# One transpose for two heads: keys and queries of a head pair turned together and spread by DMAs inside SBUF, halves of the values' products summed by GpSimd

## The chip, the cores and the metric

The kernel runs on one core of one Trainium2 chip. The metric is the device time of one execution in microseconds (us), lower is better. Inputs and output are fp32 arrays in HBM. A measurement of this kernel can tell about 0.2% (1 us) from no change.

## What is computed

Attention with rotary embedding (2 batches, 8 heads, 576 positions, 64 numbers a head), then two feed-forward layers on its 1152 tokens. The change touches the attention alone.

```python
def rotate(x):
    x1, x2 = (x[..., :half], x[..., half:])
    return np.concatenate([x1 * cos - x2 * sin, x1 * sin + x2 * cos], axis=-1)
q_rot, k_rot = (rotate(q), rotate(k))
scores = scale * np.matmul(q_rot, k_rot.transpose(0, 1, 3, 2))
scores = scores - np.max(scores, axis=-1, keepdims=True)
attn = np.exp(scores)
attn = attn / (np.sum(attn, axis=-1, keepdims=True) + 1e-09)
x = np.matmul(attn, v)
h = ((x @ w_a) * (x @ w_b) @ w_out) @ w_in
# ... SoLU and a layer norm over h, then @ w_out of the second layer
```

## The kernel before, in words

**Units and blocks.** A unit is a pair of heads of one batch: 8 units, numbered u = 0 to 7. The 2 x 576 query rows of a unit are 9 blocks of 128: blocks 0 to 3 are the first 512 rows of head 0, blocks 5 to 8 those of head 1, and block 4 holds the last 64 rows of both.

**Numbers in two parts.** TensorE multiplies in a reduced fp32 format, so each operand is written as a high part (a rounded copy, by ScalarE) and a low part (the rest, by a subtraction on VectorE or GpSimd), and a product is summed over the parts. Keys: high and low part stand above each other, 64 + 64 partitions, in `kS`. Queries: the 64 numbers stand twice above each other, once as high part and once as low part (`qS`, two slots). So one product of a block needs two weights (slots) against the same keys, each in two column halves of 288: four matmuls (L354).

**How a unit's keys and queries are made.** SP (SyncE) issues DMAs that load them (`load`, L186), GpSimd rotates them (`rope`, L224), ScalarE and GpSimd split the keys in parts (`k_hi` L262, `k_lo` L267), a DMA inside SBUF doubles the queries (`q_twice`, L242; unit 1 by GpSimd). TensorE turns them: 18 transposes of 128 x 128 a unit (`kA`, `kB` for the keys of the two heads, `qA`, `qB` for the queries, `R` for the last 64 rows; `k_tp` L284, `q_tp` L290). ScalarE copies them out of PSUM (L326, L329, and L305 with the scale for the queries' high part), VectorE makes the queries' low part (L309).

**The rest of a block.** Row maximum on VectorE (L363), exponential on ScalarE (L371), four transposes of the result (L384), high part by ScalarE (L398) and low part by VectorE (L402) into `pT`; the last 64 columns are turned by `t4A`, `t4R`, `t4B` (L408 to L420). The values' product (`pv_some`, L429) gives 128 rows: 64 from the values' high part and 64 from their low part. ScalarE copies the first 64 to SBUF (`pv_act`, L438), VectorE adds the other 64 (`pv_dve`, L443): four pieces a unit. GpSimd multiplies by the inverse row sums, which go through DRAM and come back spread by DMAs (`rs_copy`, L459), and writes the parts of x (`x_mult` L495, `x_lo` L499).

**What sets the order.** Each step has a position in a table (`PLAN`, with `FIRST`, `SECOND`, `THIRD` for units 0, 1, 2 and on), counted in blocks from the unit's start; the steps of all units are sorted by it and issued in that order. Every engine's queue, SP's DMA queue among them, runs strictly in order. The feed-forward stage after it begins near 168 us.

Of the kernel before, what the change touches and what calls it, by code (L numbers as in the profile page):

```python
# [11 lines left out]
F32 = mybir.dt.float32  # L12
# [22 lines left out]
    "qk": -0.38, "max": 0.22, "exp": 0.97, "tp": 2.23, "hi": 2.82, "lo": 3.13, "load_k": -19.75, "load_q": -16.62,  # L35
    "load_v": -7.16, "rope_k": -12.66, "rope_q": -12.07, "q2": -10.16, "k_hi": -12.41, "k_lo": -10.17, "v_hi": -2.37,
# [26 lines left out]
AB = (71.77, 72.72, 73.77, 75.49, 76.04, 76.81, 81.86, 82.31)
W_POS = (62.96, 63.3, 64.79, 65.28, 66.89, 67.84, 75.0, 76.1, 78.8)
# [45 lines left out]
def attention_gated_ffn_solu_ffn(ctx: ExitStack, tc, q, k, v, wa, wb, wo1, wi2, wo2, gln, rope_cs, out):  # L110
# [69 lines left out]
    qS = [ac.tile([P, 2, 1216], F32R, name=f"qS{i}") for i in range(2)]  # L180
    pT = ac.tile([P, 2, 9, S], F32R, name="pT")
    kS = [ac.tile([P, 2, S], F32R, name=f"kS{i}") for i in range(2)]
    kraw, vraw, kd, qd, V, qt, po = {}, {}, {}, {}, {}, {}, {}
    nm, e, sums, ps, tt, x0, rb, t2s = {}, {}, {}, {}, {}, {}, {}, {}

    def load(u, nm_, parts="ABR", eng=nc.sync):  # L186

        b, h0 = u // NP, 2 * (u % NP)  # L190
# [33 lines left out]
    def rope(eng, u, x, nm_, lo=0, hi=NB, steps=(0, 1, 2)):  # L224
# [17 lines left out]
    def q_twice(u, lo=0, hi=NB):  # L242
        dst, src = (qd[u][:, lo:hi, j, :] for j in range(2))
        if u == 1:
            nc.gpsimd.tensor_copy(dst, src)
        else:
            nc.sync.dma_start(out=dst, in_=src)

    def q_first_twice():
        nc.scalar.copy(qd[0][:, 0:5, 0, :], qd[0][:, 0:5, 1, :])  # L250

    def angles_twice():
        for t in (c_sb, s_sb):
            nc.scalar.copy(t[:, 5:9], t[:, 0:4])
# [7 lines left out]
    def k_hi(u, lo=0, hi=NB):  # L262
        if lo == 0:
            kd[u] = at.tile([P, NB, 2, D], F32R, tag="kd", name=f"kd{u}")
        copy(HI["k"] if u else "act", kd[u][:, lo:hi, 0, :], kraw[u][:, lo:hi])

    def k_lo(u, eng, lo=0, hi=NB):  # L267
        t = kd[u][:, lo:hi]
        eng.tensor_tensor(t[:, :, 1, :], kraw[u][:, lo:hi], _raw(t[:, :, 0, :]), op=ALU.subtract)
# [27 lines left out]
    def q_dst(u, piece, a, cols=slice(0, 512)):  # L297
        t = qS[u % 2]
        if piece == "R":
            return heads(t[:, a, 512:768])[:, :, 0:64]  # L300
        c0 = 0 if piece == "A" else 704
        return t[:, a, c0:c0 + 512][:, cols]

    def q_hi(u, piece, src, *cols):
        nc.scalar.activation(q_dst(u, piece, 0, *cols), src, AF.Copy, scale=1.0 / math.sqrt(D))  # L305

    def q_lo(u, piece, src, *cols):
        hi, lo = (q_dst(u, piece, a, *cols) for a in range(2))
        nc.vector.scalar_tensor_tensor(lo, src, 1.0 / math.sqrt(D), _raw(hi), op0=ALU.mult, op1=ALU.subtract)  # L309
# [625 lines left out]
```

## Time and profile before

| | |
|---|---|
| median of 3 runs | 501.88 us (501.58 to 502.71) |
| the profiled execution | 502.1 us; its span is 500.3 us |
| mean granted TensorE clock | 0.997 |
| DVE, ACT, POOL busy over the span | 75%, 54%, 30% |
| attention (units 0 to 7) | about 0 to 168 us |
| two feed-forward layers | about 168 us to the end |
| DMA | 41.72 MB, mean 83 GB/s |

A time of the trace is counted from the span's start. Busy time of PE is that of pipelined instructions, which overlap; the distance from the start of one to the start of the next is what it costs. The profiled execution is 0.2 us over the median.

### The profile page before, as it was taken

Reading aid. Unit: us, or ns where it says so; the run is one execution under the profiler, and the core shown is the slowest. Engines: PE = TensorE matmul, PEld = TensorE weight load, DVE = VectorE, ACT = ScalarE, POOL = GpSimd, SP = SyncE. Lnnn points to the kernel's source line nnn. Section 1 sums busy time; section 2 is a strip of 40 time slices with the busy share of each in tenths; the row PEclk is TensorE's granted clock in tenths of the full one; section 3 lists DMA queues with packets and bytes.
Section 4 is the critical chain, followed back from the end, with each engine's and each line's share of the span. In section 5 each row is a group of like instructions: output and inputs, shape, how many; then the busy total and the mean of one; then the engine's idle time right before and its main releaser. Section 6 shows DMA issues by size and latency. Waiting matters only on the chain.

```text
span 500.3 us, 7965 instructions
## 1 busy us (share of the span) xinstructions
PE 485.2 (97%) x3008; PEld 458.8 (92%) x3008; DVE 374.3 (75%) x603; ACT 268.7 (54%) x564; POOL 150.8 (30%) x118
## 2 busy tenths in 40 slices
PE   7699999999999999999999999999999999999997
PEld 7589999999988999999999999999999988888886
DVE  5589999999999577666756656689789898755551
ACT  3789999999988344343433433342347434222221
POOL 1997999987305002111111221100000000000000
PEclk9999999999999999999999999999999999999999
DMA  4413423424102243222232121263453100000011
GB/s 113 112 50 98 120 53 99 114 57 135 51 25 85 90 134 114 86 84 85 86 100 97 66 95 64 67 228 128 168 170 126 43 0 22 21 23 21 23 42 42
DMA packets 50804, 41.72 MB, mean 83 GB/s; under 512 B 23695, under 2 KB 46798, under 8 KB 50766
## 3 DMA queue, kind: packets, MB, share of 16 engines
q1 hardware_dynamic: 49882, 40.33, 26.5%
q10 hardware_dynamic: 884, 0.89, 0.5%
q8 instruction: 23, 0.38, 0.3%
q14 instruction: 15, 0.12, 0.1%
HBM read 36.92 MB, written 2.39 MB: 79 GB/s over the span
## 4 chain that ended last, share of the span: by engine, by line
PE 79%; DVE 8%; ACT 5%; POOL 4%; DMA 2%; issue 2%; SPq 0%; ACTq 0%; POOLq 0%; DVEq 0%
PE ab L629 28%; PE x L745 15%; PE out L863 10%; PE h L792 10%; PE pv L433 4%; PE s L354 4%; PE t L384 4%; DVE pT L402 2%; DVE nm L363 2%; PE lt L834 2%; ACT e L371 1%; ACT pT L398 1%; DVE x L447 1%; DMA kraw<-in_k_dram 1%; DMA qd<-in_q_dram 1%
## 5 line engine op out<-in xcount | busy, mean ns | idle before, releaser
L629 PE MATMUL ab<-xT,wab 128*128 128x384 f32 x864 | 151.4, 334 | 0.3 <-DVE a L638 0.3
L629 PEld LDWEIGHTS ab<-xT,wab 128*128 128x128 f32 x864 | 149.5, 188 | 0.6 <-DVE a L638 0.6
L745 PE MATMUL x<-gT,wx 128*128 128x384 f32 x432 | 75.2, 334 | 0.0
L745 PEld LDWEIGHTS x<-gT,wx 128*128 128x128 f32 x432 | 74.9, 188 | 0.1
L354 PE MATMUL s<-kS,qS 128*128 128x288 f32 x320 | 59.3, 311 | 3.6 <-ACT e L371 3.6
L106 POOL TENSOR_TENSOR wab<-f,wab 128x1024 fp32r<-128x1024 f32 x11 | 26.4, 2400 | 120.4 <-ACT wab L103 104.5
L371 ACT ACTIVATE e<-s,nm 128x576 f32<-128x576 f32 x72 | 53.5, 744 | 4.7 <-DVE nm L363 4.6
L402 DVE TENSOR_TENSOR pT<-t,pT 128x512 fp32r<-128x512 f32 x72 | 49.6, 688 | 7.6 <-ACT pT L398 6.2
L363 DVE TENSOR_REDUCE nm<-s 128x1 f32<-128x576 f32 x72 | 53.8, 748 | 1.1 <-PE s L354 1.1
L863 PE MATMUL out<-wout,lnT 128*128 128x512 f32 (+1 forms) x240 | 52.7, 372 | 0.0
L820 POOL TENSOR_TENSOR rs<-mv,mhalf 128x1 f32<-128x1 f32 x9 | 5.3, 586 | 154.8 <-DVE mv L818 154.8
L354 PEld LDWEIGHTS s<-kS,qS 128*128 128x128 f32 x320 | 45.9, 190 | 5.7 <-ACT e L371 5.2
L433 PE MATMUL pv<-pT,V 128*128 128x288 f32 x288 | 50.6, 302 | 0.2 <-DVE pT L420 0.2
L863 PEld LDWEIGHTS out<-wout,lnT 128*128 128x128 f32 x240 | 41.3, 189 | 7.4 <-DVE wout L106 0.2
L384 PE MATMUL t<-ident,e 128*128 128x128 f32 x288 | 44.3, 277 | 0.8
L398 ACT CAST pT<-t 128x512 fp32r<-128x512 f32 x72 | 41.8, 581 | 2.5 <-PE t L384 2.0
L433 PEld LDWEIGHTS pv<-pT,V 128*128 128x128 f32 x288 | 41.4, 188 | 0.7 <-POOL xT L501 0.4
L646 DVE TENSOR_TENSOR gT<-a,gT 128x384 fp32r<-128x384 f32 x36 | 23.5, 651 | 21.9 <-ACT gT L645 21.9
L637 ACT COPY a<-ab 128x384 f32<-128x384 f32 x36 | 17.3, 480 | 41.2 <-PE ab L629 40.6
L645 ACT CAST gT<-a 128x384 fp32r<-128x384 f32 x36 | 18.5, 514 | 37.4 <-DVE a L638 37.4
L384 PEld LDWEIGHTS t<-ident,e 128*128 128x128 f32 x288 | 34.0, 142 | 3.3 <-DVE pT L402 2.2
L805 ACT ACTIVATE et<-h,mx 128x1024 f32<-128x1024 f32 x9 | 10.1, 1118 | 47.8 <-DVE mx L804 47.8
(141 smaller groups left out, 739.1 us busy)
## 6 DMA issues: line engine op xcount, KB each, us to landing
raw<-in_moe_w_a_dram SPq DMA_DIRECT2D x12, 512.0 KB
raw<-in_moe_w_b_dram SPq DMA_DIRECT2D x12, 512.0 KB
raw<-in_moe_w_out_dram SPq DMA_DIRECT2D x8, 768.0 KB
raw<-in_moe_w_in_dram SPq DMA_DIRECT2D x8, 512.0 KB
raw<-in_moe_w_out_dram SPq DMA_DIRECT2D x8, 512.0 KB
kraw<-in_k_dram SPq DMA_DIRECT2D x16, 128.0 KB
qd<-in_q_dram SPq DMA_DIRECT2D x16, 128.0 KB
vraw<-in_v_dram SPq DMA_DIRECT2D x8, 256.0 KB
```

Source lines behind the costliest of these rows:

```text
L106: eng.tensor_tensor(self.w[:, 1], _raw(self.t), _raw(self.w[:, 0]), op=ALU.subtract)
L354: nc.tensor.matmul(s[:, c, :KC], qS[u % 2][:, a, off:off + P], kS[u % 2][:, h, c * KC:(c + 1) * KC], start=(m == 0), stop=(m == last),)
L363: nc.vector.tensor_reduce(t, ps[n][:, :, :KC], axis=AX.XY, op=ALU.max, negate=True)
L371: nc.scalar.activation(t.rearrange("p (c n) -> p c n", c=2), ps.pop(n)[:, :, :KC], AF.Exp, bias=nm.pop(n), accum_out=sums[u][:, i:i + 1],)
L384: nc.tensor.transpose(t[:, j, :], e[n][:, j * P:(j + 1) * P], ident)
L398: nc.scalar.copy(hi, src)
L402: nc.vector.tensor_tensor(lo, src, _raw(hi), op=ALU.subtract)
L433: nc.tensor.matmul(o[:, :KC], w[:, h, 4 if m == 8 else m % 4].rearrange("p a d -> p (a d)"), t[:, m, c * KC:(c + 1) * KC], start=(m == 0), ...
L629: nc.tensor.matmul(pab[f, t][:, m, :CW], wf[:, a, m, kk, :], xT[kk][:, xa, t * CW:(t + 1) * CW], start=(kk == a == xa == 0), stop=(kk == 3 ...
L745: nc.tensor.matmul(o[:, :CW], wx[:, a], gT[f // 3, t][:, f % 3, ga], start=(f == 0 and a == ga), stop=(f == NF - 1 and a == 1),)
L792: nc.tensor.matmul(s[:, c], x2T[kk][:, xa, c0:c0 + P], wt["h", kk][:, a, c * 512:(c + 1) * 512], start=(idx == 0), stop=(idx == 11),)
L863: nc.tensor.matmul(o[:, cols], t[:, la, kk, :], w[:, a, cols], start=(kk == la == a == 0), stop=(kk == NK2 - 1 and la == 1),)
```

## The change

For units 1 to 7 the keys and queries of both heads stand side by side (64 + 64 numbers in a row), so that one transpose turns a block of both heads: 4 for the keys (`kt`), 4 for the queries (`qt`), 3 for the last rows (`rt`), 11 in place of 18. The parts are then made from PSUM for both heads at once: high by ScalarE, low by VectorE, for the keys into `kB[0]`, `kB[1]`, for the queries into `qS[u % 2][1]`. The layout that the products need is made by 7 DMAs inside SBUF (`k_move`, 2 for each head; `q_move`, 2 and 1), all issued by SP. Block 4 uses `kB` and `qR` directly: 6 matmuls in place of 8. Two small DMAs (`shift`) bring the last rows of head 1 to the lower partitions. The values' products are copied whole (128 partitions) into `xs`, three DMAs (`x_move`) bring the halves that belong together onto the same partitions, and GpSimd adds them ahead of its multiplication. GpSimd's `k_lo`, ScalarE's `k_hi` and the DMA of `q_twice` are gone for units 1 to 7. Unit 0 keeps its way, with tables and keys in another column order; the last unit keeps VectorE's addition. All positions are new.

```diff
-    "v_lo": 5.8, "kA": (-7.65, -7.05), "qA": (-6.45, -5.8, -4.87), "R": (-1.59, -1.1, -0.66), "kB": (-3.16, -2.58),
-    "qB": (0.13, 0.57, 0.89), ...
+    "load_v": -9.48, "rope_k": -16.68, "rope_q": -10.25, "shift": (-11.47, -9.83), "v_hi": -1.05, "v_lo": 3.4,
+    "kt": (-10.76, -10.2, -8.88), "qt": (-7.29, -6.88, -5.82), "rt": (-5.65, -5.35, -4.19), "k_move": (-3.88, -1.79),
+    "q_move": (-3.26, -0.88), ...
+    "sa": 9.13, "x_move": (11.98, 15.68),
...
+    def shift(u, nm_):
+        t, last = (kraw[u % 2], 9) if nm_ == "k" else (qraw[u % 2], 10)
+        nc.sync.dma_start(out=t[0:64, last], in_=t[64:128, 8])
...
+    def kt_pe(u):
+        o = qt[u, "k"] = bank(f"kt{u}")
+        for n in range(4):
+            nc.tensor.transpose(o[:, n * P:(n + 1) * P], pair(kraw[u % 2], 2 * n), ident)
...
+    def kt_act(u):
+        nc.scalar.copy(kB[0][:, u % 2, 0:REM], qt[u, "k"])
+
+    def kt_dve(u):
+        nc.vector.tensor_tensor(
+            kB[1][:, u % 2, 0:REM], qt[u, "k"], _raw(kB[0][:, u % 2, 0:REM]), op=ALU.subtract
+        )
...
+    def k_move(u, h):
+        own, other = (LOW, HIGH)[h], (HIGH, LOW)[h]
+        t = kS[u % 2][:, h]
+        move(t[own], kB[0][own, u % 2])
+        move(t[other], kB[1][own, u % 2])
+
+    def q_move(u, h):
+        q0_, q1_ = qS[u % 2]
+        if h == 0:
+            move(q0_[LOW], q1_[LOW])
+            move(q0_[HIGH], q1_[LOW])
+        else:
+            move(q1_[LOW], q1_[HIGH])
...
+        else:
+            prods = [(qR[u % 2][:, a], kB[b][:, u % 2]) for a, b in ((0, 0), (0, 1), (1, 0))]
...
+        nc.scalar.copy(xs[u, h][:, c * KC:(c + 1) * KC], po[u, key][:, :KC])
...
+    def x_move(u, h):
+        if h == 0:
+            xs[u, 2] = at.tile([P, S], F32, tag="xs2", name=f"xs2_{u}", bufs=1)
+            nc.sync.dma_start(out=xs[u, 2][LOW], in_=xs[u, 0][HIGH])
+        else:
+            nc.sync.dma_start(out=xs[u, 0][HIGH], in_=xs[u, 1][HIGH])
+            nc.sync.dma_start(out=xs[u, 2][HIGH], in_=xs[u, 1][LOW])
...
     def x_mult(u):
+        x0[u] = xs[u, 0]
+        nc.gpsimd.tensor_tensor(x0[u], x0[u], xs[u, 2], op=ALU.add)
         nc.gpsimd.tensor_tensor(x0[u], x0[u], rb.pop(u), op=ALU.mult)
```

How the order changes, at three places. First SP's queue in the middle of the attention, before: one unit's round from the queries of unit 5 on (`rd`, `rb` are the row sums on their way through DRAM).

```order
L203 DMA qd5_1116<-in_q_dram 128x4x64 x2
L207 DMA qd5_1116<-in_q_dram 128x1x64
L466 DMA rd2_1132<-rr2_1130 9x128
L473 DMA rb2_1134<-rd2_1132 64x576
L474 DMA rb2_1134<-rd2_1132 64x512
L475 DMA rb2_1134<-rd2_1132 64x64
L212 DMA vraw4_1139<-in_v_dram 128x2x256
L217 DMA vraw4_1139<-in_v_dram 64x2x64 x2
L203 DMA kraw6_1304<-in_k_dram 128x256 x2
L207 DMA kraw6_1304<-in_k_dram 128x1x64
L247 DMA qd5_1116<-qd5_1116 128x9x64
```

The same queue with the change: the first 12 rows of a round (unit 3's keys and queries are laid out).

```order
L386 DMA kS1_99<-kB0_100 64x576
L386 DMA kS1_99<-kB1_101 64x576
L386 DMA qS1_0_104<-qS1_1_105 64x1024 x2
L255 DMA kraw0_108<-kraw0_108 64x64
L524 DMA xs0_1_790<-xs1_1_882 64x576
L525 DMA xs2_1_880<-xs1_1_882 64x576
L197 DMA kraw1_109<-in_k_dram 128x4x64 x2
L200 DMA kraw1_109<-in_k_dram 128x1x64
L386 DMA kS1_99<-kB0_100 64x576
L386 DMA kS1_99<-kB1_101 64x576
L197 DMA qraw1_111<-in_q_dram 128x4x64 x2
L200 DMA qraw1_111<-in_q_dram 128x1x64
```

A round before has 14 DMAs. With the change these 12 rows are 15, and ten more follow: L386, L255, L215, L220 x2, L542, L549, L550, L551, L522.

Second TensorE's queue in unit 3, before: `qtkB4`, `qtR4` are transposes for unit 4, `s` the products of queries and keys, `t` the transposes of the exponentials.

```order
L354 MATMUL s31_1184<-kS1_101,qS1_98 128x288 x8
L433 MATMUL pv102_1166<-pT_99,V2_702 128x288 x4
L384 MATMUL t29_1206<-ident_65,e29_1173 128x128 x4
L433 MATMUL pv112_1211<-pT_99,V2_702 128x288 x5
L354 MATMUL s32_1217<-kS1_101,qS1_98 128x288 x4
L433 MATMUL pv112_1211<-pT_99,V2_702 128x288 x4
L384 MATMUL t30_1233<-ident_65,e30_1198 128x128 x4
L354 MATMUL s33_1246<-kS1_101,qS1_98 128x288 x4
L408 MATMUL t4R3_1251<-ident_65,e31_1224 64x128
L286 MATMUL qtkB4_1255<-ident_r_102,kd4_948 128x128 x4
```

With the change, the same unit from its block 2 on.

```order
L416 MATMUL s29_1117<-kS1_99,qS1_0_104 128x288 x4
L354 MATMUL qt4_1122<-ident_65,qraw0_110 128x128 x4
L444 MATMUL t27_1127<-ident_65,e27_1091 128x128 x4
L493 MATMUL pv102_1135<-pT_97,V2_751 128x288 x9
L416 MATMUL s30_1151<-kS1_99,qS1_0_104 128x288 x4
L444 MATMUL t28_1156<-ident_65,e28_1133 128x128 x4
L359 MATMUL rt4_1171<-ident_65,kraw0_108 128x128
L359 MATMUL rt4_1171<-ident_65,qraw0_110 128x128 x2
L416 MATMUL s31_1177<-kB0_100,qRR1_107 128x288 x2
L416 MATMUL s31_1177<-kB1_101,qRR1_107 128x288 x2
L416 MATMUL s31_1177<-kB0_100,qRR1_107 128x288 x2
```

Block 4 (`s31`) goes from 8 matmuls to 6, and the last rows of unit 4 are turned in the middle of unit 3, by three transposes.

Third the start of TensorE's queue, with the change: all of unit 0's transposes (`qtkA0` to `qtqB0`) stand ahead of the first product `s0`, and unit 1's `kt1`, `qt1`, `rt1` stand among unit 0's blocks.

```order
L285 MATMUL qtkA0_204<-ident_r_114,kd0_112 128x128 x4
L291 MATMUL qtqA0_211<-ident_65,qd0_113 128x128 x4
L285 MATMUL qtR0_226<-ident_r_114,kd0_112 128x128
L291 MATMUL qtR0_226<-ident_65,qd0_113 128x128
L285 MATMUL qtkB0_240<-ident_r_114,kd0_112 128x128 x4
L291 MATMUL qtqB0_248<-ident_65,qd0_113 128x128 x4
L416 MATMUL s0_260<-kS0_98,qS0_0_102 128x288 x4
L416 MATMUL s1_268<-kS0_98,qS0_0_102 128x288 x4
L349 MATMUL kt1_275<-ident_65,kraw1_109 128x128 x4
```

Before, `qtkB0` and `qtqB0` stood behind the third product.

## Rows read from the trace of the kernel before

**Rows 1.** Stretches of one unit's length: time, each engine's busy time, clock, DMA share, GB/s
```profile
77.60:95.20 17.60, 17.50 (x142) 16.82 (x141) 16.91 (x30) 17.14 (x44) 16.61 (x14) 1.00 0.35 89
95.20:112.80 17.60, 17.50 (x142) 16.82 (x141) 16.90 (x30) 17.13 (x44) 15.75 (x13) 1.00 0.35 88
```
**Rows 2.** Timeline of PE, first products of units 1 and 7: start, length, engine, line
```profile
31.25 0.69 PE L354 MATMUL s<-kS,qS 128*128 128x288 f32 x4
...
138.60 0.69 PE L354 MATMUL s<-kS,qS 128*128 128x288 f32 x4
```
**Rows 3.** Timeline of PE inside unit 3: transposes and products
```profile
73.14 0.60 PE L292 MATMUL qtqA<-ident,qd 128*128 128x128 f32 x4
73.50 0.77 PE L354 MATMUL s<-kS,qS 128*128 128x288 f32 x4
...
74.77 0.60 PE L384 MATMUL t<-ident,e 128*128 128x128 f32 x4
75.12 1.31 PE L354 MATMUL s<-kS,qS 128*128 128x288 f32 x8
76.28 0.69 PE L433 MATMUL pv<-pT,V 128*128 128x288 f32 x4
```
**Rows 4.** Groups by shape up to 200 us: count, then total busy us and mean ns
```profile
L309 DVE SCALAR_TENSOR_TENSOR qS<-qtqB,qS 128x512 fp32r<-128x512 f32 x8 | 5.5, 692 | 0.8 <-ACT qS L305 0.5
L309 DVE SCALAR_TENSOR_TENSOR qS<-qtR,qS 128x128 fp32r<-128x128 f32 x8 | 2.3, 283 | 0.0
L447 DVE TENSOR_TENSOR x<-pv,tmp3pv 64x288 f32<-64x288 f32 x4 | 1.8, 460 | 0.1
L258 ACT CAST kd<-kraw 128x576 fp32r<-128x576 f32 x7 | 4.7, 669 | 1.5 <-POOL kraw L240 1.5
L269 POOL TENSOR_TENSOR kd<-kraw,kd 128x576 fp32r<-128x576 f32 x7 | 10.0, 1422 | 0.0
L496 POOL TENSOR_TENSOR x<-x,rb 128x576 f32<-128x576 f32 x7 | 10.0, 1424 | 0.5 <-DVE x L447 0.5
```
**Rows 5.** Timeline of POOL: one round of a unit, and a wait for a load
```profile
65.94 1.44 POOL L496 TENSOR_TENSOR x<-x,rb 128x576 f32<-128x576 f32 x1
...
81.86 1.42 POOL L496 TENSOR_TENSOR x<-x,rb 128x576 f32<-128x576 f32 x1
...
109.29 1.43 POOL L233 TENSOR_TENSOR t2q<-qd,s_sb 128x576 f32<-128x576 f32 x1 [1.42 <-DMA qd<-in_q_dram]
```
**Rows 6.** Timeline of SP's queue, one unit's round of issues
```profile
87.39 1.24 SPq L203 DMA_DIRECT2D qd<-in_q_dram  x2
...
89.34 0.41 SPq L466 DMA_DIRECT2D rd<-rr  x1
91.90 0.51 SPq L473 DMA_DIRECT2D rb<-rd  x1
92.47 0.59 SPq L474 DMA_DIRECT2D rb<-rd  x1
...
96.06 1.01 SPq L203 DMA_DIRECT2D kraw<-in_k_dram  x2
97.11 0.55 SPq L207 DMA_DIRECT2D kraw<-in_k_dram  x1
97.77 0.65 SPq L247 DMA_DIRECT2D qd<-qd  x1
```
**Rows 7.** Chain that ended last, 40 to 58 us: a load from issue to landing
```profile
41.49 3.37 DMA qd<-in_q_dram
```
**Rows 8.** Timeline of POOL at the start: unit 1's queries, then unit 0's values
```profile
12.40 1.40 POOL L233 TENSOR_TENSOR t2q<-qd,s_sb 128x576 f32<-128x576 f32 x1
...
21.08 0.72 POOL L260 CAST V<-vraw 128x640 fp32r<-128x640 f32 x1
```
**Rows 9.** Stretches of 2 us in unit 0, columns as in Rows 1
```profile
20.00:22.00 2.00, 0.28 (x2) 0.05 (x1) 0.36 (x1) 0.83 (x2) 2.00 (x3) 1.00 0.42 94
...
24.00:26.00 2.00, 1.53 (x9) 1.05 (x9) 1.97 (x4) 1.20 (x4) 2.00 (x2) 0.50 0.03 8
```

More of the change, by code (lines that the diff above doesn't have):

```diff
@@ L184, in attention_gated_ffn_solu_ffn, with load @@
+    kraw = [ac.tile([P, 10, D], F32, name=f"kraw{i}") for i in range(2)]
+    qraw = [ac.tile([P, 11, D], F32, name=f"qraw{i}") for i in range(2)]
+    kd0 = w0.tile([P, NB * P + 384], F32R, tag="w", name="kd0")
+    qR0 = kd0[:, NB * P:].rearrange("p (a n) -> p a n", a=2)
+    kd0 = kd0[:, :NB * P].rearrange("p (b a d) -> p b a d", a=2, d=D)
+    qd0 = w0.tile([P, NB, 2, D], F32, tag="w", name="qd0")
+    vraw, V, qt, po, xs = {}, {}, {}, {}, {}
     nm, e, sums, ps, tt, x0, rb, t2s = {}, {}, {}, {}, {}, {}, {}, {}
-    def load(u, nm_, parts="ABR", eng=nc.sync):
+    def load(u, nm_):
@@ L206, in load, with load_first @@
-        if "R" in parts:
-            eng.dma_start(out=t[:, 4, :], in_=src[b, h0:h0 + 2, REM:S, :])
+        src, t = (k, kraw[u % 2]) if nm_ == "k" else (q, qraw[u % 2])
+        for j in range(2):
+            nc.sync.dma_start(
+                out=t[:, j:8:2], in_=src[b, h0 + j, 0:REM, :].rearrange("(p c) d -> p c d", c=4)
+            )
+        nc.sync.dma_start(out=t[:, 8], in_=src[b, h0:h0 + 2, REM:S, :])
+    def load_first(nm_, part, eng=nc.sync):
+        src, t = (k, k0) if nm_ == "k" else (q, q0)
+        if part == "R":
+            eng.dma_start(out=t[:, 4], in_=src[0, 0:2, REM:S, :])
+        else:
+            j = "AB".index(part)
+            eng.dma_start(
+                out=t[:, 5 * j:5 * j + 4], in_=src[0, j, 0:REM, :].rearrange("(p c) d -> p c d", c=4)
+            )
@@ L260, in copy, with k_hi, k_lo @@
             {"dve": nc.vector, "pool": nc.gpsimd}[eng].tensor_copy(dst, src)
[L262 to L269, printed above, removed]
+    def k_hi(lo, hi):
+        nc.scalar.copy(kd0[:, lo:hi, 0, :], k0[:, lo:hi])
+    def k_lo(eng, lo, hi):
+        t = kd0[:, lo:hi]
+        eng.tensor_tensor(t[:, :, 1, :], k0[:, lo:hi], _raw(t[:, :, 0, :]), op=ALU.subtract)
     def v_hi(u):
@@ L294, in heads, with q_dst @@
     def heads(ap):
         return ap.rearrange("p (h n) -> p h n", h=2)
-    def q_dst(u, piece, a, cols=slice(0, 512)):
-        t = qS[u % 2]
+    def q_dst(piece, a, cols=slice(0, 512)):
         if piece == "R":
[L300 to L309, printed above, removed]
@@ L315, in qt_pe, with q_lo, q_part, first_pe @@
+    def q_lo(piece, src, *cols):
+        hi, lo = (q_dst(piece, a, *cols) for a in range(2))
+        lo_q(lo, src, hi)
+    def q_part(fn, lo, hi):
+        fn("A", qt[0, "qA"][:, lo:hi], slice(lo, hi))
+    def first_pe(u, key):
         o = bank(f"qt{key}{u}")
         if key == "R":
-            k_tp(o, u, "R")
-            q_tp(o[:, P:2 * P], u, "R")
+            k_tp(o, "R")
+            q_tp(o[:, P:2 * P], "R")
         else:
-            (k_tp if key[0] == "k" else q_tp)(o, u, key[1])
+            (k_tp if key[0] == "k" else q_tp)(o, key[1])
@@ new lines, in move @@
+    def move(dst, src):
+        nc.sync.dma_start(out=_raw(dst), in_=_raw(src))
+    LOW, HIGH = slice(0, 64), slice(64, 128)
+    def k_move(u, h):
[10 more added lines that the diff above has]
+            move(q1_[LOW], q1_[HIGH])
@@ L596, in attention_gated_ffn_solu_ffn @@
             add(plan["load_v"][0], load_v, u)
-            add(plan["rope_k"][0], lambda u: rope(nc.gpsimd, u, kraw[u], "k"), u)
-            add(plan["rope_q"][0], lambda u: rope(nc.gpsimd, u, qd[u][:, :, 1, :], "q"), u)
-            add(plan["q2"][0], q_twice, u)
-            add(plan["k_hi"][0], k_hi, u)
-            add(plan["k_lo"][0], k_lo, u, nc.gpsimd)
+            add(plan["rope_k"][0], lambda u: rope(nc.gpsimd, u, kraw[u % 2], "k"), u)
+            add(plan["rope_q"][0], lambda u: rope(nc.gpsimd, u, qraw[u % 2], "q"), u)
+            add(plan["shift"][0], shift, u, "k")
+            add(plan["shift"][1], shift, u, "q")
+            for h in range(2):
+                add(plan["k_move"][h], k_move, u, h)
+                add(plan["q_move"][h], q_move, u, h)
+            for key, fns in (("kt", (kt_pe, kt_act, kt_dve)), ("qt", (qt_pe, qt_act, qt_dve)), ("rt", (rt_pe, rt_act, rt_dve))):
+                for pos, fn in zip(plan[key], fns):
+                    add(pos, fn, u)
         for key, fn in (("v_hi", v_hi), ("v_lo", v_lo), ("sa", sums_add)):
@@ L604, in attention_gated_ffn_solu_ffn @@
         if u < NU - 1:
+            for h in range(2):
+                add(plan["x_move"][h], x_move, u, h)
             for key, fn in (("x_mult", x_mult), ("x_lo", x_lo)):
@@ L616, in attention_gated_ffn_solu_ffn @@
             for key in keys:
-                for pos, fn in zip(plan[key], (qt_pe,) if u == 0 and key == "qA" else fns):
+                for pos, fn in zip(plan[key], (first_pe,) if u == 0 and key == "qA" else fns):
                     add(pos, fn, u, key)
```

200 lines of the change are left out of this document (109 added, 91 removed), and 19 rows, old and new, of tables (FIRST, PLAN).

## Prediction, made before the changed kernel ran

> **What bounds the kernel now.** I first read the busy time in stretches of one unit's length [rows 1]. In the middle of the attention a unit takes 17.6 us, and PE (17.50), ACT (17.1) and DVE (16.9) are all busy nearly throughout; POOL has 15.75 to 16.6. No single engine is in the way: a unit gets shorter only if all three get less work and nothing else is fuller than the rest. Then I read PE's timeline for two marks [rows 2]: unit 1's first product starts at 31.25 us, unit 7's at 138.60. Six units lie between, 107.35 us or 17.9 each. What comes after 138.60 (the last unit, then the feed-forward layers, PE busy throughout) keeps its work, so I count it unchanged. Third, SP's queue [rows 6], since the change puts much there. The sum is made against the profiled execution, 502.1 us (span 500.3), which is 0.2 over the median of 501.88.
>
> **The change part by part, for one of units 1 to 7.**
>
> *PE.* 18 transposes become 11 and block 4 has 6 products in place of 8. Four transposes take 0.35 to 0.36 us from their start to the next group's (73.14 to 73.50, 74.77 to 75.12), eight products 1.16 (75.12 to 76.28) [rows 3]: 0.09 and 0.145 each. Removed: 7 x 0.09 + 2 x 0.145 = 0.92 us. PE goes from 17.5 to 16.6.
>
> *DVE.* Out go four additions of the halves at 0.46 and the three low parts of the queries, 0.69 + 0.69 + 0.28 [rows 4]: 3.50 us. In come two low parts of 512 columns, one of 128 and one of 64; the last has no row, between nothing and the 0.28 of 128 columns, I take 0.2. That is 1.86. DVE goes from 16.9 to 15.3.
>
> *ACT.* The keys' high part (0.67 [rows 4]) goes, and four copies of 512 columns become two. The four copies of the values' products now read 128 partitions in place of 64 over the same columns; nothing here says that partitions cost time. ACT ends well below PE.
>
> *POOL.* `k_lo` (1.42) goes and the addition of the halves comes, the same form and size as the multiplication beside it (1.42 [rows 4]). A round stays at 15.9 us (65.94 to 81.86 [rows 5]): hidden as long as the unit takes more.
>
> So the engines allow 16.6 us, set by PE; its lower end is POOL's 15.9, if part of PE's 17.5 is waiting that the busy time hides. Six units at 16.6 are 99.6, **7.75 us less** than 107.35.
>
> *SP's queue.* One round of a unit goes from 87.39 to 97.77, 10.38 us, for 13 DMAs, without the doubling of the queries that is dropped. It includes 2.15 in which SP stands still (89.34 + 0.41 to 91.90), because the row sums must land in DRAM before they are read back [rows 6]. The key loads come now in the pieces of the query loads: two take 1.24 in place of 1.01, so 10.6. Then come 12 more: 4 moves of keys, 3 of queries, 3 of x, 2 shifts. None is in the trace. The shortest neighbour is the 0.41 of the row sums plus a gap of 0.05: 0.46. A load with whole rows on both sides takes 0.525 with its gap (96.06 to 97.11 for two), a spread of 64 x 576 takes 0.57 (91.90 to 92.47), others 0.64, and the one DMA inside SBUF 0.65 + 0.05 = 0.70. I take 0.55, between the two rows whose shapes are nearest (whole rows; 64 x 576). A round is then 10.6 + 12 x 0.55 = 17.2 us, 0.6 more than PE's 16.6. This holds for the five units 1 to 5, where all 25 DMAs are issued; from unit 6 on the loads of keys and queries are over. 5 x 0.6 = 3.0 us of lag.
>
> Part of it is absorbed. The first moves of a unit stand 3.47 blocks ahead of its first product (positions -3.88 and -0.41), 6.4 us at 16.6 a unit; four issues (2.2) and a landing like that of the row sums (2.15) leave 2.0 us that SP may be late. So **1.0 us comes back**. The Trainium skill ("DMA: Bandwidth & Descriptors", section "Issuing engines are not separate DMA queues") says that a sequencer's time to start a DMA is usually small against the DMA itself; by that the term would be nothing. The rows speak against it: an issue is 0.4 to 0.65 us.
>
> *Behind the waiting DMAs.* `k_move` waits for ScalarE's and VectorE's parts, `shift` for GpSimd's rotation, `x_move` for the copies of the last values' products. Behind them in the same queue stand the loads of the unit after next, which have a unit of time, and the row sums, for which only POOL waits. I cost these waits at nothing as long as POOL keeps its round.
>
> *The transfers.* The moves carry 64 partitions each. The Trainium skill ("SBUF — State Buffer", section "Door 1: The DMA port swizzle") speaks against such a layout: 64 neighbouring partitions reach half of the ports, 196 GB/s against 328 at 1 MiB. By that, as an estimate, the 262 KB of a query move take 1.3 us in place of 0.8, the 2.0 us of lag allowed become 1.5, and the sum would be 0.5 us worse. No row here shows a transfer by halves of the partitions alone.
>
> *The start.* Unit 1's keys and queries are now turned inside unit 0: block 5 stands behind `rt1`, which waits for the rotation of unit 1 on POOL and for `shift`. POOL's six rotations take 8.7 us (12.40 to 21.08 [rows 8]); with an issue, a landing of 2.15 and three transposes block 5 starts near 24.1. Four blocks at 16.6 / 9 = 1.84 later unit 1 begins, at 31.5, against 31.25 now. I count no difference. At the low end it is a microsecond earlier; at the high end see the rivals.
>
> **Sum:** -7.75 + 1.0 = -6.75 us, 502.1 - 6.75 = **495.3 us**, or 495.1 from the median.
>
> **The rivals.**
> - *SP's queue has room:* at 0.46 an issue the round is 16.1, below PE, and nothing comes back: 494.4 us. For it: several issues of rows 6 are near 0.4 to 0.5. This is also what the skill's rule on issues would give.
> - *The moves land late:* a load took 3.37 us from issue to landing where other transfers stood ahead of it [rows 7]. With that in place of 2.15 the lag allowed is 0.8 and 2.2 come back: 496.5. The skill's halved ports would push the same way. Against: the DMA engines are busy only 0.35 of the time now [rows 1].
> - *POOL waits for the halves:* its addition stands ahead of the next rotations and needs the last `x_move`. If it idles 1.42 us a round, as it does once for a load [rows 5], a unit takes 17.34, and 4.4 us come back: 498.8.
> - *The start loses the clock:* PE stood idle at 20 to 22 us, and the granted clock went to 0.50 by 24 to 26, the 1.2 GHz level, after that idling [rows 9]. The new order has more waiting there (all of unit 0's transposes ahead of its first product, then the wait for `shift`). Three microseconds more are 498.3.
> - *SP's queue is the bound, and the kernel is slower:* if a DMA inside SBUF costs what the only such row does, 0.70 [rows 6], the round is 10.6 + 8.4 = 19.0. 2.4 x 5 - 2.0 = 10.0 come back: 504.4. It decides from the point where the gain is used up, (7.75 + 2.0) / 5 = 1.95 over 16.6, which is 0.66 an issue. For it: 0.64 is the most frequent step in rows 6. Against: those are spreads from DRAM and loads in pieces; the moves are whole rows on both sides, and the doubling of the queries was in 256-byte pieces.
>
> **How the numbers follow.** Forecast 0.34, SP has room 0.18, moves land late 0.10, POOL waits 0.12, start 0.08, SP is the bound 0.18. The predicted time is the forecast's, 495.3. The range takes in the lower engine bound (16.6 to 15.9 in six units, 4.2 us below 494.4, near 490) only in part and most of the last rival: 491 to 502.5, with about 0.07 below and 0.11 above. Within 0.2%, about what can be told from no change (500.9 to 502.9): 0.04 of the last rival, 0.03 of POOL's, 0.02 of the start's, together 0.09. Slower: 0.14, all from the last rival. Faster: 0.77.
>
> **What would show it right or wrong.** Right: unit 1's first product near 31 us, unit 7's near 132, units of 16.6 to 17; DVE clearly less busy than PE in a unit's stretch; SP issuing almost without a break, each new DMA about 0.5 us; the feed-forward part as long as before. Wrong: new issues of 0.65 or more and PE waiting for `kS` or `qS` at a unit's first block (SP is the bound); POOL idle ahead of its addition with a DMA as releaser (POOL); a low granted clock between 10 and 30 us and unit 1 starting after 33 (the start); or a longer time after unit 7's start, which I count as unchanged.

## The result, and the profile after

The changed kernel takes **506.66 us** (median of 4 runs, 505.27 to 507.01) against 501.73 for the kernel before in the same measurements: ratio 1.009, interval 1.0066 to 1.0113. It is slower, where 495.3 was forecast, and outside the range. The profiled execution is one of 507.01 us with a span of 505.2, so the span grew by 4.9 us.

PE's timeline gives the two marks of [rows 2], now:

```profile
33.79 0.43 PE L416 MATMUL s<-kS,qS 128*128 128x288 f32 x2
...
144.96 0.58 PE L416 MATMUL s<-kS,qS 128*128 128x288 f32 x1 [2.95 <-DMA qS<-qS]
```

Unit 1 starts 2.5 us later (33.79 against 31.25), the six units take 111.17 in place of 107.35, and what follows takes 505.2 - 144.96 = 360.2 in place of 361.7. So +2.5 + 3.8 - 1.5 = +4.8, up to rounding the whole difference. The six units take 16.56, 20.35, 18.40, 18.42, 18.42 and 19.02 us.

The stretches of a unit's length, to be read against [rows 1] (columns as there):

```profile
82.40:100.90 18.50, 16.13 (x130) 15.55 (x129) 15.04 (x27) 15.31 (x40) 15.03 (x13) 1.00 0.71 167
100.90:119.00 18.10, 16.35 (x132) 15.78 (x131) 15.26 (x27) 15.57 (x40) 15.69 (x13) 1.00 0.73 171
```

Every engine got the smaller amount of work that was forecast: PE 16.1 to 16.4 (16.6 forecast), DVE 15.0 to 15.3 (15.3), POOL 15.0 to 15.7 (15.9). Yet a unit takes 18.4 us, and the clock is full. So none of the engines is the bound. The DMA share has gone from 0.35 to above 0.7. SP's queue, one round of a unit, tells where the time goes (against [rows 6]):

```profile
82.41 0.59 SPq L522 DMA_DIRECT2D xs<-xs  x1
83.10 1.19 SPq L386 DMA_DIRECT2D kS<-kB  x2
84.34 1.23 SPq L386 DMA_DIRECT2D qS<-qS  x2
85.67 0.73 SPq L255 DMA_DIRECT2D kraw<-kraw  x1
86.51 1.24 SPq L524 DMA_DIRECT2D xs<-xs  x1
87.80 0.59 SPq L525 DMA_DIRECT2D xs<-xs  x1
88.44 1.29 SPq L197 DMA_DIRECT2D kraw<-in_k_dram  x2
...
94.58 0.54 SPq L255 DMA_DIRECT2D qraw<-qraw  x1
...
97.33 0.46 SPq L542 DMA_DIRECT2D rd<-rr  x1
99.16 0.47 SPq L549 DMA_DIRECT2D rb<-rd  x1
...
100.95 0.59 SPq L522 DMA_DIRECT2D xs<-xs  x1
```

From 82.41 to 100.95 are 18.54 us for 25 DMAs, each issued right behind the one ahead. The only pause is 1.37 us (97.79 to 99.16) for the row sums on their way through DRAM. The 12 new DMAs take 8.75 us of it with their gaps, 0.73 each; the 13 old ones 9.79 with the pause. Where nothing lengthens it, the issue of a DMA of 16 KB (L255) takes 0.54, one of 144 KB 0.59, one of 256 KB (`qS`) 0.62 with its gap: its own size hardly matters. Some issues are longer, the first `kraw` (0.73) and the `xs` behind it (1.24); the experiments come back to them. The list of SP's waits, 50 to 125 us, says the same from the other side. The kernel before had this row at the top, loads that wait for a buffer to come free (us in total, times, longest):

```profile
SPq L203 <- PE t L384: 22.8, 4, 7.0
```

That was SP's room, over 5 us a unit; the changed kernel has no such row. What PE waits for in the same stretch:

```profile
PE rt L359 <- DMA qraw<-qraw: 7.3, 4, 3.0
PE s L416 <- DMA qS<-qS: 1.0, 2, 0.7
PE s L416 <- ACT e L431: 1.0, 1, 1.0
```

`rt` are the three transposes of the last rows in the middle of a unit; they wait for `shift`, the 16 KB DMA that stands near the end of SP's round.

### The profile page after: what moved, and what is told of

Read it like the earlier page. It is cut to its first block, busy times and chain, and to the rows that moved or that the text cites. A ratio compares the mean times of both kernels' runs of the same rounds, so it can differ in the third digit from the quotient of the medians.

```text
span 505.2 us, 7965 instructions
## 1 busy us (share of the span) xinstructions
PE 478.7 (95%) x2945; PEld 455.2 (90%) x2945; DVE 364.0 (72%) x582; ACT 257.4 (51%) x542; POOL 150.9 (30%) x121
## 4 chain that ended last, share of the span: by engine, by line
PE 83%; DMA 8%; POOL 4%; ACT 2%; SPq 2%; issue 1%; DVE 0%; POOLq 0%; ACTq 0%; DVEq 0%
PE ab L720 30%; PE x L836 15%; PE out L954 10%; PE h L883 10%; PE s L416 5%; PE pv L493 5%; PE t L444 4%; DMA qraw<-qraw 3%; DMA kraw<-in_k_dram 2%; DMA qS<-qS 2%; PE lt L925 2%; DMA xs<-xs 1%; POOL xs L573 1%; POOL xs L574 1%; ACT e L431 1%
## 5 line engine op out<-in xcount | busy, mean ns | idle before, releaser
L416 PE MATMUL s<-kS,qS 128*128 128x288 f32 x256 | 49.0, 316 | 6.3 <-DMA qS<-qS 4.4
L416 PEld LDWEIGHTS s<-kS,qS 128*128 128x128 f32 x256 | 38.6, 199 | 8.4 <-issue 3.1
L728 ACT COPY a<-ab 128x384 f32<-128x384 f32 x36 | 17.2, 479 | 43.2 <-PE ab L720 42.4
L444 PEld LDWEIGHTS t<-ident,e 128*128 128x128 f32 x288 | 35.2, 143 | 0.9
```

Source lines behind the costliest of these rows:

```text
L416: nc.tensor.matmul(s[:, c, :KC], wq, mk[:, c * KC:(c + 1) * KC], start=(m == 0), stop=(m == len(prods) - 1),)
L444: nc.tensor.transpose(t[:, j, :], e[n][:, j * P:(j + 1) * P], ident)
```

## The experiments

Theory A: SP's time bounds units 1 to 5, so many issues at some 0.6 to 0.7 us whatever they carry, plus what SP stands still. Theory B: the transfers bound, bytes and pieces in flight that land late. Besides, the order on SP's queue could be at fault. All kernels are the changed one with one edit; later ones combine edits. "Six units" is the distance between the two marks in the profiled execution, "on SP" the DMAs of a round.

| run | on SP | median us | ratio to the kernel before | unit 1 | six units |
|---|---|---|---|---|---|
| before | 13 | 501.7 | | 31.25 | 107.35 |
| the change | 25 | 506.66 | 1.009 (1.0066 to 1.0113) | 33.79 | 111.17 |
| e1_x_act | 22 | 507.43 | 1.0104 (1.0082 to 1.0127) | 34.30 | 111.47 |
| e2_three_more | 28 | 517.29 | 1.0305 (1.029 to 1.032) | 34.52 | 120.63 |
| e3_half_bytes | 25 | 499.04 | 0.9946 (0.9929 to 0.9964) | 33.48 | 103.49 |
| e4_merged | 23 | 503.26 | 1.0026 (1.0007 to 1.0045) | 33.54 | 108.86 |
| e5_no_x | 22 | 501.40 | 0.9983 (0.9974 to 0.9993) | 34.32 | 104.19 |
| e6_rd_apart | 25 | 500.39 | 0.9979 (0.9955 to 1.0003) | 34.25 | 103.56 |
| e7_order | 25 | 511.77 | 1.0187 (1.0161 to 1.0214) | 33.16 | 114.49 |
| e8_all | 23 | 499.88 | 0.9953 (0.9928 to 0.9977) | 32.62 | 104.79 |
| e9_whole_rows | 25 | 504.39 | 1.0062 (1.0045 to 1.0079) | 33.11 | 107.83 |
| e10_best | 23 | 500.04 | 0.9967 (0.9947 to 0.9987) | 32.95 | 103.93 |
| e11_x_pool | 22 | 503.86 | 1.0055 (1.0021 to 1.0089) | 33.72 | 112.32 |
| e12_three_act | 25 | 510.07 | 1.0164 (1.0144 to 1.0184) | 34.22 | 114.37 |
| e13_shift | 23 | **495.21** | **0.9878 (0.9857 to 0.9898)** | 32.42 | 100.16 |
| e14_x_act_rd | 22 | 501.30 | 0.9993 (0.9971 to 1.0015) | 33.52 | 101.77 |
| e15_shift_alone | 25 | 509.13 | 1.0148 (1.0133 to 1.0163) | 33.56 | 114.38 |

The profiled execution is one run of several and can lie off the median: 4.7 us above it in e11, about 2 us below it in e9 and e14, within 1.4 us elsewhere. "Issue time" below is the sum of the lengths of a round's issues in the trace, without gaps and pauses, for three rounds in the middle of the attention; in the changed kernel it is 15.3 to 15.9 us.

**Three small DMAs more.**

```diff
+        for i in range(h, 2 * h + 1):
+            nc.sync.dma_start(out=spare[i % 2], in_=ident[0:64, 0:64])
```

> Three DMAs a unit more on SP's queue, each of 16 KB from the identity into a spare tile that nobody reads, beside the moves of the values' halves. Theory A: three issues of about 0.55 us (what the last rows' shift of the same 16 KB takes) lengthen SP's round from 18.5 to about 20.2 us; in the five or six rounds 8 to 10 us more: 514 to 517 us. Theory B: 48 KB beside 3 MB in a unit are nothing: 506 to 508 us.

517.29, 10.6 us more than the change, for 48 KB a unit. SP's rounds (from one `rd` to the next) go, in the middle of the attention, from 18.2 to between 20.1 and 20.5. Theory A is right on the count: 0.6 to 0.8 us an issue with its gap, passed on to the unit in full.

**Half the bytes.**

```diff
-        move(t[own], kB[0][own, u % 2])
+        n = S if u == 1 else KC
+        move(t[own, 0:n], kB[0][own, u % 2, 0:n])
```

(the same for the other three kinds of move)

> From unit 2 on the seven moves of keys and queries carry half their bytes (half the columns of the keys, one of the two slots of the queries; the other half of the tiles keeps an older unit's numbers); as many DMAs at the same places. 0.66 MB less a unit. Theory A: the round stays at 18.4 to 18.5 us and the time at 505 to 508 us. Theory B: landings of 3 to 4 us get shorter by up to a half, units shrink to 17 to 17.5 us: 499 to 502 us.

499.04: here Theory B's number came. Theory A's claim that bytes don't matter falls. SP's queue shows through what they act:

```profile
99.73 0.55 SPq L255 DMA_DIRECT2D kraw<-kraw  x1
100.38 0.54 SPq L526 DMA_DIRECT2D xs<-xs  x1
100.97 0.59 SPq L527 DMA_DIRECT2D xs<-xs  x1
```

The first DMA of `xs` behind the two moves of queries took 1.24 us in the changed kernel (86.51); with half the bytes it takes 0.54, and the shift ahead of it 0.55 in place of 0.73. The issue time of a round falls to 14.3 to 15.1 us, and PE's wait for the shift from 7.3 to 4.7. The pause for the row sums hardly changes (1.1 to 1.3 us, before 1.1 to 1.5). So the two theories are not rivals: what is in flight lengthens SP's round and the landings behind it.

**Fewer issues by merged loads.**

```diff
-        for j in range(2):
-            nc.sync.dma_start(out=t[:, j:8:2], in_=src[b, h0 + j, 0:REM, :]...)
+        nc.sync.dma_start(out=t[:, 0:8].rearrange("p (c j) d -> p c j d", j=2),
+                          in_=src[b, h0:h0 + 2, 0:REM, :]...)
```

> The two loads of 512 rows each (head 0 and head 1) of a unit's keys become one DMA, and so those of its queries: two issues less in a round, the same bytes in the same pieces. Theory A: if an issue costs the same however much it carries, the round falls by 2 x 0.62 = 1.2 us to 17.3: five rounds give 6 us back, 500 to 502 us. If an issue's cost grows with its pieces: unchanged, 506. Theory B: the bytes and pieces are the same, 505 to 507 us.

503.26, 3.4 us less, between the two theories. The issue of a merged load takes 0.66 us where nothing lengthens it, hardly more than one of the two before (0.60 to 0.65), but half of Theory A's gain is missing: the issue time of the 23 is 15.1 to 16.1 us, as long as that of the 25, because issues that are left got longer (two of the merged query loads take 1.40 and 2.03). So SP's round is not a count times a fixed price.

**Larger pieces in the loads.**

```diff
-                out=t[:, j:8:2], in_=...
+                out=t[:, 4 * j:4 * j + 4], in_=...
```

> The loads of a unit's 512 rows of keys and queries write head 0's and head 1's four blocks one after the other in place of alternately, so that a piece is 1 KB in place of 256 bytes; as many DMAs, as many bytes, same places and waits. The blocks that are paired in a transpose are then other rows than the reference pairs. Theory A (SP's issues): nothing changes, 505 to 508 us. Theory B (what is in flight holds up SP and the landings): the small pieces of the loads are what the moves queue behind; landings get shorter, units fall from 18.4 to 17.6 or less as when the moves carried half: 499 to 502 us.

504.39, between the two: the 256-byte pieces cost some 2 us (506.66 - 504.39), not the main part.

**The values' part undone.** `pv_act`, `pv_dve` and `x_mult` as in the kernel before, no `x_move`.

> The values' part of the change is undone (copies of 64 partitions by ScalarE, additions by VectorE, no DMA for the halves, no addition by GpSimd); the keys' and queries' part stays. Three DMAs and 0.43 MB a unit fewer, VectorE 1.8 us a unit more. Theory A (the count of DMAs on SP sets the round): the round falls from 18.4 by 2.0 to 16.4, then VectorE at about 17 us bounds: 499 to 502 us. Theory B (bytes in flight hold up SP and the landings): the 0.43 MB fewer are two thirds of what the halving took off (0.66 MB, 7.6 us less), about 5 us less: 501 to 503 us, with units of 17.7. The values' part as the cause of the loss would show as a time at or below the kernel before.

501.40, in both theories' range, so it does not tell them apart. But VectorE is all but full then, as forecast:

```profile
90.00:110.00 20.00, 19.71 (x154) 18.45 (x152) 19.58 (x35) 18.29 (x48) 16.59 (x14) 1.00 0.66 157
```

DVE is busy for 19.58 of 20 us, and PE for 19.71; a unit takes 17.4 us on average (104.19 / 6). So the room that SP gets back cannot be used much further without the values' part, and on a full SP that part costs more than it brings (506.66 against 501.40).

**The pause taken out.**

```diff
         nc.sync.dma_start(out=d, in_=rr)
+    def rs_back(u):
+        d = rd.pop(u)
...
+            add(9 * u + 14.8, rs_back, u)
```

> Nothing but an order on SP's queue: the three DMAs that spread the row sums stand 4.5 blocks behind the one that writes them to DRAM (behind one move of the values' halves, two of keys, two of queries) in place of right behind it. Theory A (SP's time): SP no longer stands still for 1.4 us in each round; units 1 to 5 go from 18.4 to 17.0, five rounds give 7 back: 499 to 501 us. Theory B (landings): the transfers are the same, 505 to 507 us. If part of the still-stand returns as issues that wait for room: 502 to 504 us.

500.39: 6.3 us less by an order alone, with the same DMAs and bytes. This is Theory A's number, but not quite by its sum. In the profiled execution units 1 to 5 give back 4.4 us (87.75 against 92.15), not 7: in most rounds SP now stands still for 0.8 to 0.9 us ahead of the key moves, and unit 3 takes 19.85 us, with a wait of PE for the shift (2.00) and half the clock behind it. Unit 6 gives another 3.2 (15.81 against 19.02), because there the pause had been 3.9 us, behind 1 MB of feed-forward weights.

**The same three DMAs on other queues.** For ScalarE `nc.scalar` in place of `nc.sync` in `x_move`, for GpSimd `nc.gpsimd`.

> The three DMAs of the values' halves of a unit are issued by ScalarE's queue in place of SP's; bytes, places and waits stay. Theory A (SP's issues are the bound: 25 in a round of 18.5 us, each about 0.6 to 0.7 us whatever its size): SP's round loses the 2.4 us that these three took and falls to about 16.1, PE's work of 16.3 to 16.6 a unit becomes the bound, about 2 us come back in each of units 1 to 5: 496 to 499 us. Theory B (the moves land late because of their bytes and their 64 partitions): the transfers are the same, 505 to 507 us. Rival to both: ScalarE pays 0.5 us an issue in its own queue and holds up the exponentials, above 507.

> The three DMAs of the values' halves are issued by GpSimd's queue in place of SP's, nothing else. They gave nothing when ScalarE's queue issued them. If ScalarE's queue was the reason (each issue held up exponentials behind it): GpSimd has 2 to 3 us a unit to spare, units fall towards 17, 498 to 502 us. If taking issues off SP does not help because the transfers are the limit: 505 to 508 us. If an issue costs GpSimd over 1 us: its 15.5 us of work become over 18.5 and the time 507 us or more.

507.43 and 503.86: nothing, and 2.8 us. In the run with ScalarE SP's round hardly got shorter: the 22 issues left take 14.3 to 15.5 us, against 15.3 to 15.9 for 25, and the pause grew in two of three rounds, here from 1.37 to 2.32 us:

```profile
96.49 0.72 SPq L542 DMA_DIRECT2D rd<-rr  x1
99.53 0.47 SPq L549 DMA_DIRECT2D rb<-rd  x1
```

The small write now stands in flight right behind the same loads. On GpSimd's queue an issue takes 0.53 us, but it waits in order for ScalarE's copies, with the next rotations behind it (this trace is of an execution of 508.61 us, so it shows the loss larger than the median has it):

```profile
85.83 0.53 POOL L524 DMA_DIRECT2D xs<-xs  x1 [3.97 <-ACT pT L476]
86.36 0.52 POOL L525 DMA_DIRECT2D xs<-xs  x1
86.89 1.45 POOL L235 TENSOR_TENSOR t2q<-qraw,s_sb 128x576 f32<-128x576 f32 x1
```

Two more runs were to tell ScalarE's own cost from the pause.

> The three spare 16 KB DMAs a unit of the earlier run, issued by ScalarE's queue in place of SP's. On SP they cost 10.6 us. If only SP's own time counts: 506 to 509 us. If ScalarE pays for an issue: 3 x 0.55 us on its 15.3 us a unit still fits into 18.4, but in the places where TensorE waits for it up to 1 us a unit comes on top, 508 to 512 us. If all queues issue through one place: as on SP, 514 to 517 us.

> Both the values' halves issued by ScalarE's queue (which gave nothing alone) and the row sums' read apart from their write (which gave 6.3 us alone). If SP's round is its issues plus its standing still, and the three issues taken away only made it stand longer for the row sums (2.4 to 3.0 us in place of 1.4): now nothing is left to stand for and units fall to 16.6 to 17, 496 to 499 us. If ScalarE's own cost of an issue was the reason: 500 to 504 us, no better than the row sums apart alone. If the transfers are the limit: 505 us or more.

510.07: an issue is not free on ScalarE's queue, but three cost 3.4 us in place of 10.6. 501.30: with the pause gone, ScalarE's issues add nothing to the row sums apart (500.39). Both fall where ScalarE's own cost was expected. In the profiled executions the last one's six units are 1.8 us shorter than with the row sums apart alone (101.77 against 103.56), but what follows unit 7's start is 1.8 us longer (362.1 against 360.3), so how the two causes share is not settled.

**Two places on SP's queue.**

```diff
-        load(1, "q")
         load(1, "k")
+        load(1, "q")
...
-    for f, loaded, steps in ((0, 54.0, W_POS[:6]), ...
+    for f, loaded, steps in ((0, 48.0, W_POS[:6]), ...
```

> Two places on SP's queue, nothing else: unit 1's keys are loaded ahead of its queries at the start, and the first feed-forward weights (1 MB) are loaded 6 blocks earlier, behind the row sums of unit 4 in place of ahead of those of unit 5. If the start and unit 6 lose what the trace shows (1.0 to 1.5 us by GpSimd's wait for unit 1's keys; 2.4 us by row sums that wait behind the weights): 502 to 504 us. If SP's count alone is behind it: 506 to 507 us.

511.77, 5.1 us worse. The start gained 0.6 (33.16). The weights, 6 blocks earlier, stand in front of unit 6's moves: unit 5 takes 22.8 us, 4.9 of them PE's wait for unit 6's queries. A place on a full queue that looks free is not.

**All of these together**, then with the weights at the start.

> Merged loads, the row sums apart and the two changed places together. Theory A: SP's round is 18.4 - 1.2 - 1.4 = 15.8 us, below TensorE's 16.6; units of 16.6 to 17.0 and the start and unit 6 without their losses: 491 to 495 us, faster than the kernel before. Theory B: transfers stay, units of 17.5 to 18: 498 to 502 us.

> As the kernel with merged loads, row sums apart and unit 1's keys first, but the first feed-forward weights (1 MB) are loaded during the start, ahead of unit 0's values, where the chip moves little, and not in unit 5. If the 20.3 us of unit 5 there came from the weights (the other units take 17.6): 2.5 to 3 us less, 496 to 498 us. If the transfers of the start are held up by them: unit 1 starts later by up to 2 us and the gain is used up, 498 to 500 us.

499.88 and 500.04: both beat the kernel before, but less than Theory A forecast (499.88 lies in Theory B's range), and moving the weights gave nothing. The cause that I had named for the first one's unit 5 (20.3 us) was wrong; PE's timeline shows another, and behind it a stretch of two us:

```profile
110.70 0.33 PE L359 MATMUL rt<-ident,qraw 128*128 128x128 f32 x1 [2.49 <-DMA qraw<-qraw]
```

```profile
112.00:114.00 2.00, 2.00 (x10) 2.00 (x10) 1.64 (x4) 1.50 (x5) 2.00 (x3) 0.50 1.08 362
```

PE waits 2.49 us for the shift, and the granted clock is at 0.50, the 1.2 GHz level, in the stretch after it. With the weights at the start the same wait and the same clock came in unit 3 (19.97 us). Its unit 4 had neither and took 16.78:

```profile
86.61:103.39 16.78, 16.26 (x133) 15.89 (x132) 15.31 (x27) 15.60 (x41) 15.61 (x12) 1.00 0.75 177
```

**The shift's place**, on this kernel and on the changed one alone.

```diff
-    "load_q": -19.13, ... "rope_q": -10.25, "shift": (-11.47, -9.83), ... "rt": (-5.65, -5.35, -4.19),
+    "load_q": -18.6, ... "rope_q": -10.7, "shift": (-11.47, -10.69), ... "rt": (-5.2, -4.9, -4.19),
```

> As the kernel with merged loads, row sums apart, unit 1's keys first and the weights at the start; now the shift of the queries' last rows stands two issues (3 DMAs with the queries' load) earlier on SP's queue, and TensorE turns the last rows half a block later. If TensorE's wait for that shift (1.2 us a unit, and the half clock after the longest of them) is what keeps units at 17 to 20 us where TensorE's work is 16.6: units 1 to 6 at 16.6 to 17.0, 493 to 497 us. If the wait only moves to the queries' slots or the keys: 498 to 501 us, as before this step.

> The changed kernel with only the shift of the queries' last rows moved earlier on SP's queue and the turn of the last rows half a block later. If SP's time a round is the bound, TensorE waits elsewhere and the units stay at 18.0 to 18.4: 504 to 507 us. If the place of that shift is the bound: units of 17, 497 to 500 us.

The queries' load stands a little later with it, and their rotation a little earlier. With room on SP it gives 495.21, ratio 0.9878: faster than both. PE's waits for DMAs in 50 to 125 us are nearly gone, and PE is busy all but throughout, in unit 4's stretch and over the six units:

```profile
PE rt L360 <- DMA qraw<-qraw: 0.2, 1, 0.2
PE s L417 <- DMA qS<-qS: 0.2, 1, 0.2
```

```profile
82.20:98.80 16.60, 16.44 (x133) 15.90 (x131) 15.75 (x28) 15.92 (x42) 15.17 (x13) 1.00 0.80 183
32.42:132.58 100.16, 98.67 (x784) 95.42 (x783) 92.39 (x157) 93.10 (x239) 81.31 (x63) 1.00 0.76 176
```

Without room on SP the same edit makes the kernel slower, 509.13, worse than either theory said. SP's queue shows where the loss comes from. The shift now stands ahead of the loads, and in unit 1 SP stands still for GpSimd's rotation, which is not done yet (timeline, then SP's waits, 28 to 50 us):

```profile
32.42 0.56 SPq L200 DMA_DIRECT2D kraw<-in_k_dram  x1
34.92 0.52 SPq L255 DMA_DIRECT2D qraw<-qraw  x1
```

```profile
SPq L255 <- POOL qraw L240: 1.9, 1, 1.9
```

The first row sums leave 2.7 us later than in the changed kernel (42.78 against 40.06), and this is never made up: the four rounds that follow take 75.65 us, against 75.50 there. With room on SP the queue stands still at the same place for 2.4 us, and unit 1 takes 17.40 in place of 16.58 without the edit; the units behind it take 16.1 to 17.7. PE's wait for the shift is gone and stands at a unit's first block instead, at times with half the clock after it (timeline, then a stretch of two us):

```profile
91.54 1.30 PE L416 MATMUL s<-kS,qS 128*128 128x288 f32 x4 [2.86 <-DMA qS<-qS]
```

```profile
92.00:94.00 2.00, 2.00 (x11) 1.98 (x11) 0.88 (x2) 0.27 (x1) 0.82 (x1) 0.50 0.67 153
```

So in the changed kernel the place of the shift was not the bound; SP's time was, and it decides where the wait falls.

## Why the prediction was wrong

The rival "SP's queue is the bound, and the kernel is slower" is what happened: SP's round sets the unit. Its price was near (0.70 a DMA, 0.73 measured) for another reason, and that its 504.4 lies close to 506.66 is in part luck, since the losses of the start and of unit 6 aren't in it. Step by step:

- **PE 16.6, DVE 15.3, POOL 15.9 a unit: right.** The busy times above and the six units of 16.69 on average (100.16) in the best kernel show that the term of -7.75 was there to be had, nearly whole: 107.35 - 100.16 = 7.19. That the best kernel's 495.21 equals the forecast is luck: it is another kernel, with 1.2 us lost at the start and 1.4 gained after unit 7's start.
- **12 x 0.55 on SP: too small, this step failed.** Measured 8.75 in place of 6.6, 0.73 each, past the rival's deciding point of 0.66. A move alone is 0.6; the rest is single issues of 0.7 to 1.24, mostly behind large moves, which no row of before showed. The 13 old DMAs took 9.79 in place of 10.6, since the pause was shorter. Units 1 to 5 took 18.43 on average in place of 17.2: 1.23 x 5 = 6.15 us.
- **The 2.0 us that SP may be late: not there, the second failing step.** I measured the slack at the first moves of a unit. The transfer that PE waits for is another, the shift of the last rows (60.65: 2.98 us, and three more times), issued late in the round and used in the middle of a unit. Units 1 to 5 took 92.15 where 5 x 16.6 are 83.0: 9.15 us came back, not 1.0. That is the 3.0 of lag that the sum had, the 6.15 above, and nothing absorbed.
- **The start "no difference": wrong by 2.5 us.** POOL's rotations of unit 1 begin at 14.85, not 12.40 as in [rows 8], because the keys are loaded behind the queries (POOL's timeline); block 5 came at 26.61 (PE's timeline), forecast was 24.1:

```profile
14.85 1.40 POOL L235 TENSOR_TENSOR t2k<-kraw,s_sb 128x576 f32<-128x576 f32 x1 [1.56 <-DMA kraw<-in_k_dram]
```

```profile
26.61 0.77 PE L416 MATMUL s<-kS,qS 128*128 128x288 f32 x4
```

  With the loads exchanged unit 1 starts at 33.16, 0.6 of the 2.5 us. The rival on the clock was right in part: PE stood idle from 8 to 12 us, and the clock is at 0.50 from 12 to 16 and 0.52 up to 18 ([rows 9] had it at 24 to 26). What of the rest is the clock was not tried alone. The stretches of two us of the start:

```profile
10.00:12.00 2.00, 0.00 (x0) 0.00 (x0) 1.90 (x5) 0.76 (x2) 0.29 (x1) 0.77 0.66 150
12.00:14.00 2.00, 1.92 (x12) 1.93 (x13) 0.02 (x1) 0.85 (x3) 1.29 (x2) 0.50 0.50 113
```

- **Unit 6, not in the sum: 19.02, 2.4 over 16.6.** The row sums' write stands right behind 1 MB of weights, and SP stands still 3.9 us for it, with unit 7's moves behind (SP's timeline):

```profile
131.19 0.51 SPq L141 DMA_DIRECT2D raw<-in_moe_w_b_dram  x1
131.80 0.37 SPq L542 DMA_DIRECT2D rd<-rr  x1
136.11 0.47 SPq L549 DMA_DIRECT2D rb<-rd  x1
```

  I had counted waits behind the row sums at nothing as long as POOL keeps its round; with a full SP they cost all that is queued behind.
- **Unchanged after unit 7's start: nearly**, 360.2 against 361.7.

The terms add up: -7.75 + 9.15 + 2.4 + 2.5 - 1.5 = +4.8 us, against 4.9 measured.

The rival "the moves land late" had a part too: half the bytes gave 7.6 us back. POOL's wait for the halves exists, but POOL had the time: in the best kernel it stands idle for `xs` for 9.4 us in four waits (50 to 125 us), and the units there take 16.2 to 17.7.

On the Trainium skill: "DMA: Bandwidth & Descriptors", section "Issuing engines are not separate DMA queues", says that the sequencer's time to start a DMA is usually small against the DMA, and that DMAs from all engines run on the same DMA engines. The first is so here for one DMA (0.54 us of issue, over 3 us to the landing of a shift), but it doesn't make the issues negligible: three of 16 KB a unit cost 10.6 us. The second fits the runs on ScalarE's and GpSimd's queues, where taking three DMAs off SP gave 0 and 2.8 us. "Perfetto Trace Analysis", section "What "DMA-bound" means", names an issuing engine that is solid with DMA issues as a bound of its own; that is what SP's round shows. Whether 64 partitions make a transfer slower was not tried: the halved moves kept their partitions. And how the loss divides between the count of issues and what is in flight stays open, since each run that took issues or bytes away changed the lengths of the issues left.

## What to carry to other kernels

Count DMAs per queue and round, with the pauses, as one counts an engine's busy time: at 0.6 us an issue and more behind large moves, a queue of 25 was the bound of an 18 us round in which every engine had 2 us to spare. Where a queue is nearly full, first take out what it stands still for (a read right behind the write that it waits for: 6.3 us), then issues, and only then move single transfers earlier: the same move gave 4.8 us on a queue with room and cost 2.5 on a full one, where the queue stood still for it. Slack is to be measured at every transfer that an engine uses next, the smallest too, not at the one that comes first.

## What the runs showed of the hardware that I had not expected

- Most issues take 0.46 to 0.66 us from 4.5 KB to 256 KB, but some take twice that. Whatever DMA stands second behind the two 256 KB moves of queries does: a move of `xs` 1.20 to 1.25 in the changed kernel, a spare one of 16 KB 1.29 to 1.33 with three DMAs more, a read of row sums 1.28 to 1.34 with the row sums apart (below, timeline of SP; `xs` is back at 0.54 there). When the two moves carry half, it takes 0.54.

```profile
79.94 1.23 SPq L386 DMA_DIRECT2D qS<-qS  x2
81.27 0.62 SPq L552 DMA_DIRECT2D rb<-rd  x1
81.94 1.34 SPq L553 DMA_DIRECT2D rb<-rd  x1
```

- A 16 KB transfer inside SBUF with loads ahead of it was used 3 to 5 us after its issue began: in the changed kernel issued at 94.58, and PE went on at 97.78; in the run with all edits together issued at 106.07, and PE went on at 110.70.
- Waits of PE of 2.5 to 3 us in the middle of the attention were often followed by a granted clock of 0.50, as at 110.70 and 91.54 above, but not always: after the one of 2.98 us at 60.65 in the changed kernel the clock stayed full in the stretch after it. What makes the difference is open.

```profile
62.00:64.00 2.00, 2.00 (x19) 1.90 (x17) 2.00 (x5) 1.88 (x7) 2.00 (x2) 1.00 0.17 62
```
